# Loading four thirds of q, k and v ahead into hT's space, U by one DMA and TensorE, weight chunks in order of need, and batch 1 transposed on TensorE

## The chip, the cores and the metric

The kernel runs on one core of a Trainium2 chip. The metric is the device time of the whole kernel in microseconds (us); lower is better. Each kernel was timed in turns with the kernel before on the same chip.

The engines: TensorE (PE in the profile, PEld for its weight loads), VectorE (DVE), ScalarE (ACT), GpSimd (POOL) and SyncE (SP), which issues most DMAs. SBUF is the on-chip memory, PSUM the small memory that TensorE writes.

## The reference

Attention with normalised q and k, then a low-rank mixer over the sequence and a two-layer MLP with residual. Shapes: q, k, v are (8, 12, 448, 64); U is (448, 32), V (32, 448), w_ch1 (768, 3072), w_ch2 (3072, 768), all float32.

```python
q_n, k_n = rmsnorm(q, g_q), rmsnorm(k, g_k)
attn = softmax(q_n @ k_n.T / sqrt(64)) @ v       # per batch and head
x = attn.transpose(0, 2, 1, 3).reshape(8, 448, 768)
h = x.transpose(0, 2, 1) @ U @ V
u = x + h.transpose(0, 2, 1)
out = u + relu(u @ w_ch1) @ w_ch2
```

## The kernel before

The work on q, k and v goes by *thirds* (four heads of one batch; third `t` belongs to batch `t // 3`) and by *pairs* (two heads; pair `p` belongs to third `p // 2`). The *head* is the attention of batch 0, pairs 0 to 5, with the start of pair 6. Its loop has one step for each pair p, and the step for pair p also scales pair p + 2. After it, batch b's MLP fills TensorE while batch b+1's attention is woven in between. Six "chunks" each of w1 and w2 are loaded by GpSimd's queue.

```python
NE, NV, NWARM, NH = 2, 3, 16, 3
FA, FM, NPE = 0.77, 0.09, 8        # FA: the share of an MLP that the next attention is spread over
loads = ctx.enter_context(tc.tile_pool(name="loads", bufs=2))      # two thirds of q, k; two of v

def load_mix():                    # U, in 14 small DMAs
    Ur = moe_U.rearrange("(p j) r -> j p r", j=NJ)
    for par in range(2):
        for i, off in enumerate(OFFS[par]):
            lo, hi = max(off, 0), min(off + P, S)
            for j, p0, p1, r in segments(lo, hi):
                r += lo - off
                nc.sync.dma_start(Uf[r:r + p1 - p0, par, i, :], Ur[j, p0:p1, :])
    nc.sync.dma_start(Vf, ...)

def squares(t, hs=ALL, ss=(0, 1)):
    for s in ss:
        ...
        if t < 3:
            nc.scalar.activation(sqs[t, s][:, hs], qks[t][:, s, hs], AF.Square)
        else:
            nc.gpsimd.tensor_tensor(sqs[t, s][:, hs], qks[t][:, s, hs], qks[t][:, s, hs], OP.mult)

def scale(t, pr):                  # "the scaling": q and k times 1/rms, two VectorE instructions a pair
    ...
    for s in range(2):
        nc.vector.tensor_tensor(qkns[t][:, pr, s]..., qk[:, s, hp]...,
                                rstd[:, s, hp]....to_broadcast([SP, 2, NJ, D]), OP.mult)

def transposes(p):
    ...
    if p < NPE:                    # eight TensorE transposes and two evictions
        ...
    else:                          # one DMA transpose
        nc.sync.dma_start_transpose(qkT.rearrange("d s (j p) -> d (s j) p", j=NJ), qkn)
```

In the head's loop a third is loaded (`load(t + 3)`, `load_v(t + 3)`) when the buffer that it takes is free, and w1 chunks 2 to 5 go out at pairs 1 and 2. All six w2 chunks are issued together behind the head.

## Time and profile before

| | before |
|---|---|
| time, median of 3 runs | 659.18 us (659.03 to 661.39) |
| span of the profiled run | 659.2 us |
| TensorE busy | 599.2 us (91%) |
| first MLP matmul of batch 0 (the head's end) | 74.09 us |
| first matmul with w2 | 121.32 us |
| first MLP matmul of batch 1 | 154.28 us |
| from there to the end | 504.9 us |

Three lines of the page's second part: the span in 40 slices of 16.5 us. A digit is the busy share of a slice in tenths; PEclk is TensorE's granted clock in tenths of full speed; DMA is the mean busy share of the 16 DMA engines.

```profile
PE   5286895999999999899999999899999999999997
PEclk8688896999999999999999999999999999999999
DMA  6999697554443625564443534563444331030011
```

After the seventh slice TensorE is nearly always busy, so only the first 150 us have time to give. There the DMA engines are the busy ones. The timeline of TensorE (start in us, length, engine, line, what, count, and in brackets how long the engine had been idle and on whom it waited) shows the gaps:

```profile
20.37 0.40 PE L213 MATMUL sc<-qkT 64*112 64x448 bf16 x2 [0.92 <-ACT E_95 L218]
32.58 0.62 PE L213 MATMUL sc<-qkT 64*112 64x448 bf16 x2 [11.81 <-ACT E_95 L218]
...
50.65 1.04 PE L237 MATMUL o<-va_98,E_95 112*128 112x65 bf16 x16 [3.04 <-DVE t4b L296]
...
66.07 1.04 PE L237 MATMUL o<-va_99,E_95 112*128 112x65 bf16 x16 [3.98 <-DVE t4b L296]
...
74.09 1.14 PE L319 MATMUL ph<-u_367,w1b 128*128 128x384 bf16 x6
...
109.75 1.00 PE L213 MATMUL sc<-qkT 64*112 64x448 bf16 x4 [7.94 <-DVE qkT L205]
```

Gaps of 11.8, 3.0, 4.0 and 7.9 us. The bracket names the last engine in a chain, not the cause. The cause is in the chain of waits (start, length, what), followed back through the same time:

```profile
13.32 0.48 SPq L114
...
16.81 0.66 SPq L115
...
17.59 13.05 DMA qk<-in_q_dram
...
30.66 1.06 ACT sq L162
...
91.83 17.41 DMA qkT<-qkn
```

L114 is the line of U's 14 loads. Third 2 of q was issued at 17.59 us behind them and took 13.05 us to land; ScalarE's squares, and through them all that follows, waited for it. The last line is a DMA transpose of q and k that needed 17.41 us, issued while the six w2 chunks were loading.

### The profile page before, as it was taken

The numbers are of one execution on the slowest core, as the hardware profiler recorded it, in microseconds if no ns is written. First come the engines' busy times: TensorE is split into PE (matmuls) and PEld (weight loads), VectorE is DVE, ScalarE is ACT, GpSimd is POOL, SyncE is SP. The second block draws the span as 40 slices with busy tenths as digits, with TensorE's granted clock in tenths as the row PEclk, the third lists the DMA queues.
The fourth block names the chain that finished last, engine by engine and source line by source line (L and its number), as shares of the span: only waits on it lengthen the run. The fifth ranks groups of instructions, "written<-read, shape, count | busy, mean of one in ns | idle before, by whom it ended". The sixth has DMA issues, their size and how long they took to land.

```text
span 659.2 us, 11159 instructions
## 1 busy us (share of the span) xinstructions
PE 599.2 (91%) x4700; PEld 329.7 (50%) x4700; DVE 338.8 (51%) x737; ACT 233.9 (35%) x347; POOL 117.2 (18%) x96
## 2 busy tenths in 40 slices
PE   5286895999999999899999999899999999999997
PEld 2043452554445555554456555554456555554464
DVE  4257862664555546673645456673645456352211
ACT  4264252413553055414453056414543065402100
POOL 3024602220211202320220203320221200000000
PEclk8688896999999999999999999999999999999999
DMA  6999697554443625564443534563444331030011
GB/s 145 214 186 182 136 216 147 113 134 99 98 105 78 136 53 112 112 152 82 106 106 96 112 67 98 123 156 66 112 98 118 89 68 29 25 73 25 0 49 49
DMA packets 104534, 68.64 MB, mean 104 GB/s; under 512 B 60836, under 2 KB 100900, under 8 KB 104484
## 3 DMA queue, kind: packets, MB, share of 16 engines
q1 hardware_dynamic: 96292, 58.49, 39.0%
q0 software_dynamic: 7872, 9.44, 8.6%
q8 instruction: 37, 0.61, 0.4%
q14 instruction: 13, 0.11, 0.1%
q10 hardware_dynamic: 320, 0.00, 0.0%
HBM read 52.25 MB, written 11.01 MB: 96 GB/s over the span
## 4 chain that ended last, share of the span: by engine, by line
PE 77%; DMA 9%; DVE 8%; ACT 2%; issue 1%; SPq 1%; POOL 1%; DVEq 0%; POOLq 0%
PE po L334 32%; PE ph L319 30%; PE o L237 7%; PE sc L213 6%; DMA qk<-in_q_dram 4%; DVE qkn L184 3%; DMA qkT<-qkn 3%; DVE osb L338 1%; DMA vt<-in_v_dram 1%; DVE rstd L170 1%; PE pu L276 1%; ACT hT L322 1%; ACT E_96 L218 1%; DVE hT L324 1%; ACT E_95 L218 1%
## 5 line engine op out<-in xcount | busy, mean ns | idle before, releaser
L334 PE MATMUL po<-w2b,hT 128*128 128x384 bf16 x1344 | 235.2, 326 | 2.9 <-DVE osb L338 2.9
L334 PEld LDWEIGHTS <-hT 128*128 128x128 bf16 x1344 | 126.3, 98 | 92.5 <-issue 15.0
L319 PEld LDWEIGHTS <-w1b 128*128 128x128 bf16 x1152 | 106.7, 98 | 106.7 <-issue 17.6
L164 POOL TENSOR_TENSOR sq<-qk 112x1024 f32<-112x1024 f32 x42 | 79.0, 1896 | 370.9 <-DMA qk<-in_q_dram 354.0
L322 ACT ACTIVATE hT<-ph 128x384 bf16<-128x384 f32 (+1 forms) x96 | 52.3, 545 | 252.5 <-PE ph L319 252.5
L218 ACT ACTIVATE E_96<-sc 112x896 bf16<-112x896 f32 x96 | 85.6, 914 | 71.1 <-PE sc L213 71.1
L324 DVE TENSOR_SCALAR hT<-ph 128x384 bf16<-128x384 f32 (+1 forms) x96 | 59.8, 623 | 92.0 <-PE ph L319 91.4
L218 ACT ACTIVATE E_95<-sc 112x896 bf16<-112x896 f32 x96 | 85.4, 912 | 42.4 <-PE sc L213 42.3
L213 PE MATMUL sc<-qkT 64*112 64x448 bf16 x384 | 61.9, 384 | 29.9 <-DVE qkT L205 14.7
L184 DVE TENSOR_TENSOR qkn<-qk,rstd 112x512 bf16<-112x512 f32 x96 | 70.5, 774 | 17.9 <-ACT rstd L176 17.3
L170 DVE TENSOR_REDUCE rstd<-sq 112x16 f32<-112x1024 f32 (+1 forms) x50 | 58.2, 1167 | 23.8 <-ACT sq L162 15.5
L213 PEld LDWEIGHTS <-qkT 64*112 64x112 bf16 x384 | 21.5, 128 | 69.1 <-issue 56.8
L240 DVE RECIPROCAL rec<-o 128x4 f32<-128x4 f32 x96 | 17.2, 180 | 52.0 <-PE o L237 51.9
L237 PEld LDWEIGHTS <-E_95 112*128 112x128 bf16 x768 | 31.7, 101 | 16.1 <-issue 10.6
L237 PEld LDWEIGHTS <-E_96 112*128 112x128 bf16 x768 | 30.1, 98 | 11.8 <-DVE xs_100 L244 3.0
L319 PE MATMUL ph<-u_5020,w1b 128*128 128x512 bf16 x144 | 33.3, 379 | 0.0
L319 PE MATMUL ph<-u_1608,w1b 128*128 128x512 bf16 x144 | 33.3, 379 | 0.0
L319 PE MATMUL ph<-u_3314,w1b 128*128 128x512 bf16 x144 | 33.3, 379 | 0.0
L319 PE MATMUL ph<-u_6686,w1b 128*128 128x512 bf16 x144 | 31.2, 379 | 0.0
L319 PE MATMUL ph<-u_367,w1b 128*128 128x384 bf16 x144 | 28.1, 343 | 1.0 <-ACT hT L322 0.5
L319 PE MATMUL ph<-u_5889,w1b 128*128 128x384 bf16 x144 | 25.8, 326 | 0.0
L319 PE MATMUL ph<-u_2477,w1b 128*128 128x384 bf16 x144 | 25.6, 326 | 0.0
(100 smaller groups left out, 383.2 us busy)
## 6 DMA issues: line engine op xcount, KB each, us to landing
vt<-in_v_dram SPq DMA_DIRECT2D x24, 448.0 KB, 6.6
qk<-in_q_dram SPq DMA_DIRECT2D x23, 448.0 KB, 4.3
qk<-in_k_dram SPq DMA_DIRECT2D x23, 448.0 KB, 5.7
w1b<-in_moe_w_ch_dram POOLq DMA_DIRECT2D x6, 768.0 KB, 9.4
w2b<-in_moe_w_ch_dram POOLq DMA_DIRECT2D x6, 768.0 KB, 17.3
out_dram<-osb SPq DMA_DIRECT2D x8, 336.0 KB, 2.8
out_dram<-osb SPq DMA_DIRECT2D x8, 288.0 KB, 3.0
out_dram<-osb SPq DMA_DIRECT2D x8, 240.0 KB, 2.6
```

The source lines that it names most:

```text
L164: nc.gpsimd.tensor_tensor(sqs[t, s][:, hs], qks[t][:, s, hs], qks[t][:, s, hs], OP.mult)
L170: nc.vector.tensor_reduce(rstds[t][:, s, hs].rearrange("p h j -> p (h j)"), sqs[t, s][:, hs].rearrange("p h (j d) -> p (h j) d", d=D), AX, ...
L184: nc.vector.tensor_tensor(qkns[t][:, pr, s].rearrange("p j h d -> p h j d"), qk[:, s, hp].rearrange("p h (j d) -> p h j d", d=D), rstd[:, ...
L213: nc.tensor.matmul(sc[:, hh, 0:S], kT[pp, kc * SP:(kc + 1) * SP], qT[pp, :], start=True, stop=True)
L218: nc.scalar.activation(Es[p % NE][:, :, PAD + kc * S:PAD + (kc + 1) * S], scs.pop((p, kc))[:, :, 0:S], AF.Exp, scale=float(D) ** 0.5)
L237: nc.tensor.matmul(o[:, i, :], E[:, hh, c:c + P], va[:, hl, kc, :], start=(kc == 0), stop=(kc == NJ - 1))
L240: nc.vector.reciprocal(rec, o[:, :, D])
L276: nc.tensor.matmul(pu, lhsT, t4s[b][:, hs], start=True, stop=True)
L319: nc.tensor.matmul(ph, w1b[:, dc, hc * P:(hc + 1) * P], u[:, dc, :], start=(dc == 0), stop=(dc == KD - 1))
L322: nc.scalar.activation(hT[:, hc, 0:n], ph, AF.Relu)
L324: nc.vector.tensor_relu(hT[:, hc, 0:n], ph)
L334: nc.tensor.matmul(po, hT[:, hc, i * P:(i + 1) * P], w2b[:, hc, hs], start=(hc == 0), stop=(hc == KH - 1))
```

## The change

Its intent: to have data in SBUF before it is needed. While hT (the MLP's hidden layer, 24 KiB per partition) is unused in the head, thirds 2 and 3 are loaded into its space, so four thirds are issued at once. U comes by one DMA and is put in shape by TensorE transposes. w1 chunks go out one by one at pairs 1 to 4, w2 chunks three after the head and three at pairs 8 to 10. Pairs 8 to 11 (batch 1) are transposed on TensorE (NPE 12), and batch 1's attention is spread over half of batch 0's MLP (FA0 = 0.5) so that w2 may come later. Third 2's squares move from ScalarE to GpSimd, and one PSUM copy (mix_b) from VectorE to ScalarE.

```diff
+    spare = hT.rearrange("p k n -> p (k n)").bitcast(FP32).rearrange("p (t s h e) -> p t s h e", t=2, s=3, h=HG)
-    FA, FM, NPE = 0.77, 0.09, 8
+    FA, FM, NPE, FA0 = 0.77, 0.09, 12, 0.5
... (U: one DMA into Uf [112, 128]; setup_u and setup_v: cast, 4 + 8 TensorE transposes, two copies;
     the four small loads of g_q and g_k become two)
     def load(t, parts=1):
-        qks[t] = loads.tile([SP, 2, HG, NJ * D], FP32, tag="qk", name="qk")
+        if t in (2, 3):
+            qks[t] = spare[0:SP, t - 2, 0:2]
+        else:
+            qks[t] = loads.tile([SP, 2, HG, NJ * D], FP32, tag="qk", name="qk")
... (load_v the same)
-            if t < 3:
+            if t < 2:
                 nc.scalar.activation(sqs[t, s][:, hs], qks[t][:, s, hs], AF.Square)
             else:
                 nc.gpsimd.tensor_tensor(...)
... (mix_b)
-        nc.vector.tensor_copy(us[b][:, dc, :], pu)
+        nc.scalar.activation(us[b][:, dc, :], pu, AF.Copy)
... (attention)
-            if t + 2 < NT:
-                add(0, reduce, t + 2, ALL, (odd,))
+            if t + 2 < NT and p != 8:
+                add(0, reduce, t + 2, ALL, (0, 1) if p == 9 else (odd,))
+            if 8 <= p <= 10:
+                add(0, load_w2, p - 5)
... (head: loads first; pair 0 reordered; load(p + 4) at pairs 0 and 1)
         load(0, 2)
         load(1)
         load_v(0)
+        load(2)
+        load_mix()
+        load_v(1)
+        load_v(2)
+        load(3)
+        load_v(3)
         setup()
... (pair 0)
+                squares(1)
+                squares(2)
...
-            if p in (1, 2):
-                load_w1(2 * p)
-                load_w1(2 * p + 1)
+            if 0 < p < 5:
+                load_w1(p + 1)
... (main)
-        for i in range(6):
+        for i in range(3):
             load_w2(i)
-                weave(fill, total * FA, attention(b + 1) if b else rest)
+                weave(fill, total * (FA if b else FA0), attention(b + 1) if b else rest)
```

More of the change, by code (lines that the diff above doesn't have):

```diff
@@ L97, in setup, with setup_u, setup_v @@
             nc.gpsimd.memset(t, 0.0)
-        nc.gpsimd.memset(Uf, 0.0)
+        nc.gpsimd.memset(UT, 0.0)
         nc.gpsimd.memset(Vsh, 0.0)
-        for half in range(2):
-            nc.scalar.dma_start(gg[half * D:(half + 1) * D, :], g_q.rearrange("(d o) -> d o", o=1))
-            nc.scalar.dma_start(gk2[half * D:(half + 1) * D, :], g_k.rearrange("(d o) -> d o", o=1))
-    Uf = consts.tile([P, 2, 4, rank], FP32, name="Uf")
+        for t, g in ((gg, g_q), (gk2, g_k)):
+            nc.scalar.dma_start(t, g.rearrange("(a d o) -> a d o", a=1, o=1).to_broadcast([2, D, 1]))
+    Uf = consts.tile([SP, NJ * rank], FP32, name="Uf")
+    Uc = consts.tile([SP, NJ * rank], BF16, name="Uc")
+    UT = consts.tile([rank, PAD + S + PAD], BF16, name="UT")
     Vf = consts.tile([P, S], FP32, name="Vf")
     def load_mix():
-        Ur = moe_U.rearrange("(p j) r -> j p r", j=NJ)
+        nc.sync.dma_start(Uf, moe_U.rearrange("(p j) r -> p (j r)", j=NJ))
+        nc.sync.dma_start(Vf, moe_V.rearrange("r s -> () r s").to_broadcast([4, rank, S]))
+    def setup_u():
+        nc.vector.tensor_copy(Uc, Uf)
+        pt = ps_mm.tile([rank, S], BF16, tag="mm")
+        for j in range(NJ):
+            nc.tensor.transpose(pt[:, j * SP:(j + 1) * SP], Uc[:, j * rank:(j + 1) * rank], ident[:SP, :SP])
+        nc.vector.tensor_copy(UT[:, PAD:PAD + S], pt)
+    def setup_v():
+        pt = ps_mm.tile([P, 2, 4, rank], BF16, tag="mm")
         for par in range(2):
             for i, off in enumerate(OFFS[par]):
-                lo, hi = max(off, 0), min(off + P, S)
-                for j, p0, p1, r in segments(lo, hi):
-                    r += lo - off
-                    nc.sync.dma_start(Uf[r:r + p1 - p0, par, i, :], Ur[j, p0:p1, :])
-        nc.sync.dma_start(Vf, moe_V.rearrange("r s -> () r s").to_broadcast([4, rank, S]))
-    def setup_mix():
-        nc.vector.tensor_copy(Ub, Uf)
+                nc.tensor.transpose(pt[:, par, i, :], UT[:, PAD + off:PAD + off + P], ident[:rank, :rank])
+        nc.vector.tensor_copy(Ub, pt)
         nc.vector.tensor_copy(V4.rearrange("r (j p) -> r j p", j=NJ), Vf.rearrange("r (p j) -> r j p", j=NJ))
@@ L147, in load_v @@
         b, h0 = t // 3, (t % 3) * HG
-        vt = loads.tile([SP, HG, NJ * D], FP32, tag="vt")
+        if t in (2, 3):
+            vt = spare[0:SP, t - 2, 2]
+        else:
+            vt = loads.tile([SP, HG, NJ * D], FP32, tag="vt", name="vt")
         nc.sync.dma_start(vt, v[b, h0:h0 + HG].rearrange("h (p j) d -> p h (j d)", j=NJ))
@@ L396, in head @@
         reduce(0, A)
-        squares(0, Bh)
+        squares(0, Bh, (0,))
         rsqrt(0, A)
+        squares(0, Bh, (1,))
+        reduce(0, Bh, (0,))
         scale(0, 0)
@@ L401, in head @@
         transposes(0)
-        reduce(0, Bh)
+        reduce(0, Bh, (1,))
         rsqrt(0, Bh)
-        squares(1)
-        scale(0, 1)
-        load_mix()
-        load(2)
-        load_v(1)
-        load_v(2)
         cast_v(0)
@@ L412, in head @@
         load_w1(1)
+        scores(0, (0, 1))
         for p in range(7):
             t, odd = divmod(p, 2)
-            scores(p, (0, 1))
+            if p > 1:
+                scores(p, (0, 1))
             expo(p, 0)
@@ L418, in head @@
                 mix_a(0, p - 2)
+            if p == 0:
+                scale(0, 1)
             transposes(p + 1)
+            expo(p, 1)
             if p == 0:
-                reduce(1)
-            expo(p, 1)
-            if not odd:
+                squares(1)
+                squares(2)
+            elif not odd:
                 rsqrt(t + 1)
@@ L430, in head @@
                 mix_a(0, 5)
-            elif p < 6:
+            elif p:
                 heat(NH)
@@ L440, in head @@
                 mix_b(0, p - 2)
+            if p == 0:
+                scores(1, (0, 1))
+            expo(p, 3)
+            if p == 0:
+                reduce(1)
+                rsqrt(1)
             scale(t + 1, odd)
             if p == 1:
-                setup_mix()
-            squares(t + 2, ss=(odd,))
-            expo(p, 3)
-            reduce(t + 2, ss=(odd,))
+                setup_u()
+                setup_v()
+            if p > 1:
+                squares(t + 2, ALL, (odd,))
+            reduce(t + 2, ALL, (odd,))
+            if p < 2:
+                load(p + 4)
+                load_v(p + 4)
             if p < 6:
@@ L450, in head @@
                 cast_v(t + 1)
-                load(t + 3)
-                load_v(t + 3)
-            if p in (1, 2):
-                load_w1(2 * p)
-                load_w1(2 * p + 1)
+            if 0 < p < 5:
+                load_w1(p + 1)
     def mixing(b):
```

## The prediction

> **What bounds the kernel now.** From 154 us (batch 1's MLP starts, by the timeline) to the end TensorE is busy in 99 to 100% of nearly every slice (page, part 2); the change leaves those 505 us alone. Before that the core is starved. TensorE's timeline: warm-up until 10 us, the head (batch 0's attention) until 74 us, then batch 0's MLP with batch 1's attention until 154 us. The chain of waits runs here over DMA landings: U and v issues until 17.6 us, third 2 of q (13.05 us), 7.4 us (third 3), 7.6 us (third 4), 17.4 us (a DMA transpose). TensorE stands still 11.8 us at 20.8 to 32.6, about 3 us at 47, 4 us at 62, and 7.9 us at 102 to 110. The granted clock falls to 0.66-0.76 around them (windows of 10 us).
>
> Why the loads are late: 14 small U loads hold SyncE from 5.7 to 16.8 us, each waiting for an older DMA; thirds 3 and 4 are issued at 39.7 and 54.9 us, after a buffer is free. The DMA transposes of pairs 8 to 11 queue behind six w2 chunks issued together at 75.7 us.
>
> **What the change does.**
> - U: 14 loads become one; 12 TensorE transposes and small copies (each under 0.6 us) are added.
> - Thirds 0 to 3 issued by about 14 us; third 2 should land near 20 us instead of 31: most of the 11.8, 3 and 4 us stalls go. Its squares move to GpSimd (1.9 us each instead of 1.05).
> - mix_b's copy (0.54 us a pair) goes from VectorE, 97% busy at 50 to 60 us, to ScalarE.
> - Pairs 8 to 11: TensorE transposes (0.37-0.56 us a pair) and two evictions (0.45 + 0.38 us, for a 0.34 us gain). Removes the 7.9 us stall and some 3 us of slow clock.
> - w2 chunks are spread; batch 1's attention goes into the first half of batch 0's MLP. Neutral in TensorE work.
>
> **Floor.** In the first 120 us the queues took 56.6 us (47.2%) for 12 weight chunks and 46.4 us for eight thirds with the rest: 103 of 120 us. The Trainium skill, "DMA: Bandwidth & Descriptors" (Queues, rings and completion order) says that each DMA engine takes the queue rows in turn; the trace agrees: third 2, sharing with two w1 chunks, took 13.05 us against 3.4 us for the first loads. So the second matmul can't start before about 95 us (121 now).
>
> **Estimate.** Head: pair 2 starts near 31 us (39.5 now); pairs 2 to 6 need 5.2 us each (34.6 us now less 8.5 us of stalls): end at 57 us instead of 74. Batch 0's MLP part: 80 us less 8, 3 and about 1: 69 us, plus 0 to 4 us waiting for the last w2 chunk or third 7. Batch 1's MLP starts at 126 to 131 us instead of 154: 24 us won, nearly all critical.
>
> **Prediction: 635 us, 8 in 10 between 627 and 646.** Faster by over 2%: 0.91; within 2%: 0.08; slower: 0.01.
>
> **What would show it.** No TensorE gap above 4 us at 20 to 33 us; thirds 3 and 4 landed before use; VectorE busiest in the head, 5.2 us a pair; head end 54 to 62 us; no DMA transpose of q/k before 100 us; first po matmul at 96 to 106 us; last 505 us unchanged.
>
> **What would make it wrong.** Weight chunks delaying third 2 or 4 (head end near 65); GpSimd waiting for third 7 and so issuing the last w2 chunk late (5 to 10 us at the first po group); VectorE or ScalarE too dense when five pairs go into half the MLP; a slower steady state from shifted loads.

## More of the kernel before

One more reading, not looked at closely before the prediction, matters later: VectorE's time in the scalings (line L184 of this kernel), in two stretches, by the view of busy time by windows filtered to that line. The columns are window, length, VectorE's time with the count, clock, DMA share, GB/s.

```profile
0.00:74.10 74.10, 11.83 (x16) 0.79 0.85 173
74.10:142.00 67.90, 9.43 (x12) 0.92 0.80 161
```

28 scalings in 21.26 us.

## The result, and the profile after

The result is correct. The median is 644.41 us (643.31 to 645.25, 4 runs) against 659.11 us of the kernel before beside it: ratio 0.9768, 95% interval 0.9742 to 0.9795. A ratio here and below is the mean time of one kernel's runs over that of the other's runs of the same rounds, so not quite the ratio of the medians. Executions over 1.5% slower than the fastest of the same kernel are left out of the means. 14.7 us were won; 24 had been predicted. The time lies inside the stated range, near its slow end.

| | before | predicted | after |
|---|---|---|---|
| head's end | 74.1 us | 57 us | 62.6 us |
| from there to batch 1's MLP | 80.2 us | 69 to 73 us | 72.3 us |
| from there to the end | 504.9 us | the same | 506.6 us |
| span of the profiled run | 659.2 us | | 641.5 us |

(The traced execution of before took 661.1 us, one of its slower ones, that of after 643.3 us, its fastest, so the traces differ by 17.7 us, the medians by 14.7.)

The same lines of the page:

```profile
PE   5688988999999999899999999899999999999996
PEclk9689999999999999999999999899999999999999
DMA  9999797325346455444155355353355321040011
```

The DMA engines are busy without a break through the first four slices, and TensorE's second slice, a 2 before, is a 6. Its timeline:

```profile
28.55 0.37 PE L118 MATMUL pt<-ident,Uc 112*32 112x112 bf16 x4 [2.13 <-DVE Uc L115]
...
62.58 1.25 PE L333 MATMUL ph<-u_371,w1b 128*128 128x384 bf16 x6
...
85.53 0.55 PE L211 MATMUL pt<-ident,qkn 112*128 112x112 bf16 x8 [1.32 <-DVE hT L338]
...
100.90 2.11 PE L333 MATMUL ph<-u_371,w1b 128*128 128x384 bf16 x12 [1.62 <-DVE hT L338]
...
134.92 1.46 PE L333 MATMUL ph<-u_1558,w1b 128*128 128x512 bf16 x6
```

No gap is longer than 2.2 us after the start. All four gaps of before are gone. And yet the head ended 5.6 us later than estimated. The releaser in the brackets is VectorE now, and VectorE's scalings (L198 in this kernel) have become longer:

```profile
0.00:62.60 62.60, 18.83 (x17) 0.84 1.09 223
62.60:110.00 47.40, 13.39 (x12) 1.00 0.84 168
```

32.22 us for the same 28 scalings that took 21.26 us before (one lies across the border and is counted in both windows). In the chain of waits of the first 160 us the scalings are 15.1%; before it was 3.2%. Most of the DMA waits left the chain (the loads of q are 3.5% of it now, 17.6% before) and something that makes VectorE slow entered it. Line by line, in the head's step for pair 2, which scales pair 4 (one answer of the timeline, all engines, cut to GpSimd and the scaling; a pair's two scalings are one line):

```profile
35.90 1.88 POOL L178 TENSOR_TENSOR sq<-hT 112x1024 f32<-112x1024 f32 x1 [0.96 <-DMA hT<-in_k_dram]
...
36.09 3.68 DVE L198 TENSOR_TENSOR qkn<-hT,rstd 112x512 bf16<-112x512 f32 x2
...
37.74 1.49 POOL L167 CAST va_99<-hT 112x1024 bf16<-112x1024 f32 x1
```

The pair of scalings takes 1.27 to 1.29 us when alone and 3.68 us here. It started 0.2 us after GpSimd's square. 35.90 + 1.88 is 37.78: the first scaling seems to stand until the square ends, the second until the cast of v ends (37.74 + 1.49 = 39.23). This pattern fits the Trainium skill, "SBUF — State Buffer" (Who interferes with whom): "A DVE instruction with two SBUF inputs contends with a GpSimd instruction that reads SBUF", one engine holding a shared read interface for a whole instruction and the other blocked. The scaling has two SBUF inputs, q or k and rstd.

### The profile page after: what moved, and what is told of

Same layout as the page of the kernel before. It is cut to its first block, busy times and chain, and to the rows that moved or that the text cites. A ratio compares the mean times of both kernels' runs of the same rounds, so it can differ in the third digit from the quotient of the medians.

```text
span 641.5 us, 11220 instructions
## 1 busy us (share of the span) xinstructions
PE 599.3 (93%) x4741; PEld 330.7 (52%) x4741; DVE 349.7 (55%) x737; ACT 234.4 (37%) x351; POOL 122.1 (19%) x98
## 4 chain that ended last, share of the span: by engine, by line
PE 80%; DVE 13%; ACT 3%; DMA 2%; issue 1%; SPq 0%; DVEq 0%; ACTq 0%
PE po L348 33%; PE ph L333 29%; PE o L251 7%; PE sc L227 7%; DVE qkn L198 6%; DVE rstd L184 1%; DVE osb L352 1%; ACT E_95 L232 1%; PE pu L290 1%; DVE hT L338 1%; DMA qkT<-qkn 1%; DMA qk<-in_q_dram 1%; PE warm L509 1%; PE pt L211 1%; ACT E_96 L232 1%
## 5 line engine op out<-in xcount | busy, mean ns | idle before, releaser
L348 PEld LDWEIGHTS <-hT 128*128 128x128 bf16 x1344 | 127.3, 98 | 93.6 <-issue 15.8
L333 PEld LDWEIGHTS <-w1b 128*128 128x128 bf16 x1152 | 105.9, 98 | 105.8 <-issue 16.6
L178 POOL TENSOR_TENSOR sq<-qk 112x1024 f32<-112x1024 f32 x40 | 75.4, 1892 | 353.6 <-DMA qk<-in_q_dram 317.9
L232 ACT ACTIVATE E_96<-sc 112x896 bf16<-112x896 f32 x96 | 85.9, 913 | 65.7 <-PE sc L227 65.7
L198 DVE TENSOR_TENSOR qkn<-qk,rstd 112x512 bf16<-112x512 f32 x88 | 71.4, 851 | 16.5 <-ACT rstd L190 16.0
## 6 DMA issues: line engine op xcount, KB each, us to landing
w1b<-in_moe_w_ch_dram POOLq DMA_DIRECT2D x6, 768.0 KB, 15.1
```

Of the source, the lines that this page charges most:

```text
L198: nc.vector.tensor_tensor(qkns[t][:, pr, s].rearrange("p j h d -> p h j d"), qk[:, s, hp].rearrange("p h (j d) -> p h j d", d=D), rstd[:, ...
L232: nc.scalar.activation(Es[p % NE][:, :, PAD + kc * S:PAD + (kc + 1) * S], scs.pop((p, kc))[:, :, 0:S], AF.Exp, scale=float(D) ** 0.5)
L333: nc.tensor.matmul(ph, w1b[:, dc, hc * P:(hc + 1) * P], u[:, dc, :], start=(dc == 0), stop=(dc == KD - 1))
L348: nc.tensor.matmul(po, hT[:, hc, i * P:(i + 1) * P], w2b[:, hc, hs], start=(hc == 0), stop=(hc == KH - 1))
```

## The experiments

The theory: in the kernel before, GpSimd's squares came when a late load had just landed, and VectorE was mostly idle then, waiting for the same load. With the loads early, GpSimd's reads fall on VectorE's scalings, and VectorE, which sets the pace of the head, stands still for them. The rivals: (1) the scalings are slow because thirds 2 and 3 lie in hT's space; (2) the denser DMA traffic slows VectorE; (3) GpSimd being busy at all slows it. A second question is what each part of the change is worth: the head's part (early loads, U, w1 order) and the second part (TensorE transposes of batch 1, w2 spread, FA0).

Runs of one batch ran on the same chip: the first four below, the next four, the last four.

### The head's part alone

```diff
-    FA, FM, NPE, FA0 = 0.77, 0.09, 12, 0.5
+    FA, FM, NPE, FA0 = 0.77, 0.09, 8, 0.77
-            if t + 2 < NT and p != 8:
-                add(0, reduce, t + 2, ALL, (0, 1) if p == 9 else (odd,))
+            if t + 2 < NT:
+                add(0, reduce, t + 2, ALL, (odd,))
-            if 8 <= p <= 10:
-                add(0, load_w2, p - 5)
-        for i in range(3):
+        for i in range(6):
             load_w2(i)
```

> The head's part of the change alone (early loads, U by one DMA, weight order, w1 spread, mix_b's copy on ScalarE); pairs 8 to 11 again by DMA transposes, w2 chunks all issued at once, batch 1's attention over 0.77 of batch 0's MLP. Theory (the two parts add up): the head ends at about 62.6 us as in the full change, so 11 us are won there, and the stall behind the w2 chunks (7.9 us before) comes back: 648 to 651 us. Rival (the head's gain is given back later because the loads collide with w2): over 654 us. If the second part is worth nothing: 644 us.

Measured: 644.33 us, ratio 0.9759 (0.9742 to 0.9777): no slower than the whole change. In its trace the head ends at 58.6 us, 4 us sooner than in the trace of the whole change although the head's code is the same, and the scalings meet GpSimd at other places (3.34 us at 18, 3.20 at 46, 5.00 at 58). The last of them does not fit the pattern wholly (GpSimd's line L140 issues the six w2 chunks):

```profile
56.03 4.52 POOL L140 DMA_DIRECT2D w2b<-in_moe_w_ch_dram  x6
58.04 5.00 DVE L198 TENSOR_TENSOR qkn<-qk,rstd 112x512 bf16<-112x512 f32 x2
60.53 1.95 POOL L178 TENSOR_TENSOR sq<-qk 112x1024 f32<-112x1024 f32 x1
```

The pair's first scaling takes 2.04 us although GpSimd only issues weight chunks beside it. Elsewhere scalings beside such issues take 0.67 us (at 42.4 us in the run with the squares of thirds 3 to 7 on ScalarE, for one). What held this one is not shown. The wait for the DMA transpose came back, but smaller:

```profile
92.27 0.59 PE L227 MATMUL sc<-qkT 64*112 64x448 bf16 x4 [3.12 <-DVE qkT L219]
```

3.1 us, not 7.9. So the head's part carries the gain, and the second part adds nothing that these two results can tell apart. My expectation of 648 to 651 us was wrong.

### The second part alone, on the kernel before

```diff
-    FA, FM, NPE = 0.77, 0.09, 8
+    FA, FM, NPE, FA0 = 0.77, 0.09, 12, 0.5
+            (the reduce, load_w2 and weave lines of the change)
```

> The second part alone on the kernel before: pairs 8 to 11 transposed on TensorE, w2 chunks spread over pairs 8 to 10, attention of batch 1 pressed into the first half of batch 0's MLP. Theory: the head still ends at 74 us, and the 80 us after it become about 72, as in the full change: 651 to 653 us. Rival (it only pays when the w1 chunks are early): 656 to 660 us.

Measured: 658.35 us, 0.9966 (0.993 to 1.0002): at most a little faster. The 7.9 us gap at 102 us is gone from its trace, but the stretch from the head's end (74.3 us) to batch 1's MLP (151.8 us) is 77.5 us against 80.2: three of its pairs of scalings take 4.1 to 4.4 us (at 75, 98 and 113 us), while no pair in the kernel before took more than 2.15 before 110 us. What the part takes out of the DMA waits it gives back, for the most part, in VectorE's waits.

### Squares of thirds 2 to 7 on ScalarE

```diff
-            if t < 2:
+            if t < 8:
                 nc.scalar.activation(sqs[t, s][:, hs], qks[t][:, s, hs], AF.Square)
```

> The changed kernel with the squares of thirds 2 to 7 on ScalarE (1.05 us each) instead of GpSimd (1.9 us each). Theory (GpSimd reading SBUF holds up VectorE's scaling, which has two SBUF inputs): the 28 scalings before 110 us take 19 to 21 us in sum instead of 32.2 (28 at 0.65 would be 18), the head ends 3 to 6 us sooner, total 636 to 642 us. Rival 1 (scalings that read third 2 and 3 from hT's space are slow for their place): those 8 keep a median near 1.4 us. Rival 2 (DMA writes slow VectorE): all stay near 32 us in sum. If ScalarE's 13 us more become the limit: scalings short, yet 644 us or more.

Measured: 640.52 us, 0.9709 (0.9681 to 0.9736). The same view of the scalings:

```profile
0.00:60.40 60.40, 10.77 (x17) 0.86 1.11 226
60.40:110.00 49.60, 8.07 (x12) 0.97 0.79 168
```

The 14 pairs of scalings before 110 us take 18.8 us: thirteen of them 1.27 to 1.30 us, one 2.14 (beside a cast of v, which stays on GpSimd). Those that read hT's space are as short as the others, which is against rival 1. The DMA engines' share in the head is no lower (1.11 against 1.09), which is against rival 2. The head ends at 60.4 us only, because ScalarE does third 2's squares ahead of pair 0's exponentials now and TensorE waits 5.6 us for those at 20 us. In total the run is faster than the change's first ratio (0.9768), but its interval overlaps that of the change's second run below (0.9734, 0.9701 to 0.9766): that the shorter scalings win time here is likely, not settled.

### The scaling's second input in PSUM

rstd is put in the unused end of the PSUM bank of o. GpSimd keeps all its work.

```diff
+    ob = ps_o.tile([P, 512], FP32, tag="o", name="ob")
-            rstds[t] = norm.tile([SP, 2, HG, NJ], FP32, tag="rstd", name="rstd", bufs=3)
+            c = 384 + 32 * (t % 3)
+            rstds[t] = ob[0:SP, c:c + 32].rearrange("p (s h j) -> p s h j", s=2, h=HG)
-            o = ps_o.tile([P, 4, D + 1], FP32, tag="o")
+            o = ob[:, 0:4 * (D + 1)].rearrange("p (c e) -> p c e", c=4)
```

> The changed kernel with the scaling's second input (rstd) in PSUM, in the unused end of the bank of o; GpSimd does what it did. Theory (the two SBUF inputs are what collides): the 28 scalings take 18 to 21 us in sum instead of 32.2 although GpSimd's squares run at the same times, the head ends 3 to 6 us sooner, total 635 to 641 us. Rival 1 (place in hT) and rival 2 (DMA writes): sum stays near 32 us, total 644 us. Rival 3 (GpSimd busy at all slows VectorE): stays near 32 us too.

Measured: 647.3 us, 0.9799 (0.9778 to 0.9821), slower than the change's two runs (644.41 and 643.43 us; all four executions are above all eight of those); but the scalings did what the theory said. The same two views (scalings by windows; the timeline at the same place):

```profile
0.00:62.00 62.00, 11.17 (x18) 0.83 1.10 226
62.00:110.00 48.00, 6.72 (x11) 1.00 0.82 160
```

```profile
35.04 1.88 POOL L179 TENSOR_TENSOR sq<-hT 112x1024 f32<-112x1024 f32 x1 [1.07 <-DVE rec L256]
...
35.40 1.27 DVE L200 TENSOR_TENSOR qkn<-hT,ob 112x512 bf16<-112x512 f32 x2
```

The scalings start in the middle of GpSimd's square and take 1.27 us, as if alone. This is no matter of luck in timing: 12 of the 28 overlap a square or a cast of GpSimd in this trace (10 in the changed kernel's first trace, most of them stretched, up to 3.74 us). All 28 together take 17.89 us, each between 668 and 689 ns, with the same DMA share (1.10 in the head), the same place in hT and the same GpSimd work. That leaves none of the three rivals: what collides is the second SBUF input. This is the cleanest of the runs for the mechanism.

The time was lost elsewhere, in part before and in part after 110 us. The view of waits up to 110 us (engine, tile and line, waited for whom: us in total, times, longest) has lines that the changed kernel has no match for:

```profile
PE ob L253 <- ACT ob L192: 6.4, 5, 1.8
...
PE ob L253 <- DVE ob L186: 2.9, 4, 1.4
PE ob L253 <- DVE qkn L200: 2.1, 3, 0.8
```

o and rstd share one tile now, and TensorE's write of o waits for engines that only work on rstd: 11.4 us in sum. The cure for one wait made another. A further 3.3 us are lost from batch 1's MLP to the end (509.9 us in this trace against 506.6 in the changed kernel's first); their cause was not looked for.

### The changed kernel once more

No edit.

> The changed kernel once more, unedited, to have it on the same chip as the next three and to see a second trace. Theory (GpSimd's reads meet VectorE's scalings whenever a load happens to land just before one): the sum of the 28 scalings before 110 us differs from the first trace's 32.2 us by some us and the head's end moves with it, between 58 and 63 us; the time stays at 0.975 to 0.979 of before. Rival (the collisions are fixed by the program): the same pairs collide, sum within 1 us of 32.2, head end 62 to 63 us.

Measured: 643.43 us, 0.9734 (0.9701 to 0.9766), single runs from 640.35 to 644.81. The head ends at 57.6 us in this trace, 5 us sooner than in the first, from the same program; head's end and ratio lie just outside what I expected (58 to 63 us, 0.975 to 0.979). The place of the collision shown above looks like this here:

```profile
36.82 3.04 POOL L178 TENSOR_TENSOR sq<-hT 112x1024 f32<-112x1024 f32 x1 [1.00 <-DVE x L255]
36.83 1.27 DVE L198 TENSOR_TENSOR qkn<-hT,rstd 112x512 bf16<-112x512 f32 x2
```

The two start within 0.01 us and now it is GpSimd that takes longer: 3.04 us instead of 1.88, by about the 1.2 us of the scalings. So a shift of a fifth of a microsecond goes with a change of who waits. The skill's page says that issue order, not the shape of the operation, decides who blocks. These traces agree that the same two operations can end either way, but their recorded starts do not show the order: here the square is recorded first, by 0.01 us, and yet waits, and the scaling at 93.90 us below is recorded 0.72 us ahead of a square and takes 4.16 us. GpSimd was off the critical path there, so when it loses, nothing is lost: in the steps for pairs 2 to 5 the scalings all take 1.27 us in this trace and the head is 5 us shorter. In the second stretch this execution was less lucky: 5.55 us for the pair at 75.75 us, behind two squares and a cast in a row, and 4.76 us for the one at 93.9. Head's end to batch 1's MLP is 75.7 us against 72.3. The sum of scalings is 29.1 us.

### Squares of thirds 3 to 7 on ScalarE, third 2 on GpSimd

```diff
-            if t < 2:
+            if t < 8 and t != 2:
```

> The changed kernel with the squares of thirds 3 to 7 on ScalarE and those of third 2 left on GpSimd (ScalarE is needed for pair 0's exponentials then). Theory: sum of the scalings 20 to 22 us (one collision of about 2.5 us at 18 us stays), pairs 2 to 6 of the head 5.2 to 5.4 us each, head end 57 to 59 us, total 2 us below the run with all squares of thirds 2 to 7 on ScalarE: 0.967 to 0.970 of before. Rival (the head is no longer bound by VectorE): head end near 60.4 us as in that run and 0.971.

Measured: 641.0 us, 0.970 (0.968 to 0.972). The sum of scalings is 20.7 us, with one collision left (4.01 us at 18 us), pairs 2 to 6 of the head are 5.3 us apart as estimated from the kernel before (5.2), and the head ends at 59.3 us, 1.1 us sooner than with all of them on ScalarE. One trace of each does not settle 1.1 us, and the totals (0.970 and 0.9709) can't be told apart.

### The same with batch 1's attention over 0.6 of batch 0's MLP

```diff
-    FA, FM, NPE, FA0 = 0.77, 0.09, 12, 0.5
+    FA, FM, NPE, FA0 = 0.77, 0.09, 12, 0.6
```

> The same with batch 1's attention over 0.6 instead of 0.5 of batch 0's MLP. Theory (between 62 and 110 us TensorE waits because VectorE is 88% busy when five pairs are pressed into half the MLP): TensorE's idle time from the head's end to batch 1's MLP falls from about 6 us to 3 us, total 2 to 3 us under sq_act37, 0.963 to 0.967 of before. Rival (w2 chunks, issued with pairs 8 to 10, come later than the second matmul now): a wait of 3 us or more at the first po group, same or slower than sq_act37.

Measured: 637.54 us, 0.9652 (0.9634 to 0.967), 3.5 us under the run with 0.5 by the medians. The stretch after the head is 71.5 us against 73.3, and no wait for w2 shows at the first matmul with w2 (101.6 us). So 0.6 is better than 0.5, but not by the way I expected: without the collisions VectorE was only 73% busy there with 0.5 (37.3 of 50.7 us), and what TensorE waited for most was ScalarE's exponentials (3.1 us, now 1.6). TensorE's idle time in the stretch fell from 5.4 to 4.4 us, not to 3, and the two traced executions differ by 1.1 us only; where the rest of the 3.5 us was won is not shown. (0.77 with the change's w2 order was refused by the check before any run: w2 would be read before its last chunk is issued.)

### The U part alone, on the kernel before

```diff
-  (14 DMAs of U, cast to Ub)
+  (setup_u, setup_v and load_mix of the change)
```

> The U part alone on the kernel before: one DMA, TensorE transposes, copies; order of the other loads, buffers and NPE as before. Theory (the 14 small loads held the issue of third 2 from 7 to 17.6 us): third 2 is issued near 7 us and lands before 21 us, the TensorE gap of 11.8 us at 20.8 us falls below 4 us, the 3 and 4 us gaps at thirds 3 and 4 stay, since those loads still wait for a buffer: 7 to 9 us faster, 0.986 to 0.989 of before. Rival (w1 chunks are what makes third 2 late): gap still over 8 us, 0.995 to 1.0.

Measured: 653.56 us, 0.9883 (0.9836 to 0.993). The size was as expected, the way there was not. Third 2 was issued at 14.77 us, not at 7, because its buffer is third 0's and is free only when pair 1 has been scaled:

```profile
13.18 1.54 DVE qkn L191
...
14.77 5.30 DMA qk<-in_q_dram
```

So the U loads (and V behind them) held it for 2.8 us only (17.59 less 14.77; within the trace of the kernel before pair 1's scaling ends at 15.25 us, which makes it 2.3). But those 2.8 us were the ones in which GpSimd issued two w1 chunks (14.6 to 16.5 us in the kernel before) and SyncE the load of V: here the first chunk went out at 14.10 us, the second at 15.11 and V long before. Issued between the chunks, third 2 landed in 5.30 us; behind both, V and the last U loads in 13.05. Which of these counts for how much is not shown. The gap at 20.8 us shrank from 11.8 us to 1.8. The head ended at 65.7 us. The 3 us gap at third 3 went, that at third 4 stayed (3.7 us), and TensorE waited 3.2 us at 28 us for U's cast, which it did not before. The gap behind the w2 chunks stayed (8.64 us at 94 to 102 us).

### All squares of thirds 2 to 7 on ScalarE, third 2's placed later

```diff
-            if t < 2:
+            if t < 8:
...
                 squares(1)
-                squares(2)
...
                 rsqrt(1)
+                squares(2)
...
-    FA, FM, NPE, FA0 = 0.77, 0.09, 12, 0.5
+    FA, FM, NPE, FA0 = 0.77, 0.09, 12, 0.6
```

> Squares of thirds 2 to 7 all on ScalarE, those of third 2 placed after pair 0's exponentials and the next rsqrt (ScalarE idled 5.6 us there), attention of batch 1 over 0.6 of batch 0's MLP. Theory: the collision at 18 us (4.2 us for a pair of scalings instead of 1.3) goes too, sum of the 28 scalings 18 to 19 us, head end 56.5 to 58.5 us, total 2 to 3 us under the last best: 0.960 to 0.964 of before. Rival (the exponentials of pair 1, now 2 us later, hold up the head as much): head end near 60 us, 0.965.

Measured: 634.13 us (632.51 to 635.13), 0.9594 (0.9569 to 0.962), correct. The scalings:

```profile
0.00:55.20 55.20, 10.95 (x18) 0.90 1.10 227
55.20:110.00 54.80, 7.05 (x11) 0.97 0.88 182
```

17.99 us in sum, no collision left; the head ends at 55.2 us, batch 1's MLP starts at 126.4. In the chain of waits of the first 160 us the scalings are 2.4%. Against the change's two ratios (0.9768 and 0.9734) that is 9 to 11.5 us of 660, with the same loads as in the change. Not all of it is the collisions: FA0 differs too. Against the run with 0.6 and third 2's squares on GpSimd (0.9652, 0.9634 to 0.967) only those two squares differ, and with them the one collision left (4.22 us for that pair instead of 1.29): the head ends 4.8 us sooner (55.2 against 60.0) and the ratio falls by 0.6% with intervals apart.

### The same with 0.66

> The same with 0.66. Theory (attention and the last w2 chunk move together, since chunk 5 is issued with pair 10): TensorE has less VectorE work per time in the first half, 1 us more gained. Rival: the second matmul now starts so soon after chunk 5's issue that TensorE waits 3 to 6 us for it; then slower than with 0.6.

Measured: 632.88 us (631.3 to 636.66), 0.9587 (0.9542 to 0.9632). The intervals of the two overlap almost wholly: 0.66 is no worse and not shown to be better. TensorE shows no wait over 1.2 us between 26 us and batch 1's MLP but one (1.23 us at 54 us), so the rival's wait for w2 did not come.

### The head's part alone, squares of thirds 3 to 7 on ScalarE

The edit of the first experiment together with `t < 8 and t != 2`.

> The head's part of the change alone (as the earlier run of it) with the squares of thirds 3 to 7 on ScalarE: what the second part (TensorE transposes of pairs 8 to 11, w2 spread, attention in half the MLP) is worth when collisions no longer blur it, against 0.970 with the second part. Theory (the second part removes a 3 us wait for a DMA transpose and was masked by collisions it brought itself): 0.973 to 0.976. Rival (it is worth nothing once third 2 to 4 are early): 0.968 to 0.971.

Measured: 642.61 us, 0.9728 (0.9704 to 0.9751). With the second part the same squares gave 0.970 (0.968 to 0.972), in another batch. The wait for a DMA transpose is 6.2 us in this trace (at 86 to 92 us). So with the collisions mostly out of the way the second part looks worth about 0.3%, 2 us; the intervals overlap, so this is likely and not settled.

### The changed kernel with U by 14 loads

> The changed kernel with U by 14 small DMAs and casts as before, at the place in the queue that the one DMA has. Theory (small DMAs hold SyncE, each waits for an older one): v of third 1 and 2 and third 3 are issued 6 to 10 us later, pair 2 waits for v or third 3, head end 64 to 68 us, 0.982 to 0.988 of before. Rival (with third 2 already issued ahead of them the small loads cost nothing): 0.973 to 0.977.

The result of this kernel is wrong, and by my mistake, not on purpose: in the changed order the loads come ahead of GpSimd's clearing of U's tile, so the clearing, which waits 18.6 us for them, zeroes U. The mistake also changes the timing. GpSimd's queue is held until 22.1 us, and with it the first cast of v (22.6 us instead of 14.0) and the first two w1 chunks (issued from 23.6 us instead of 15.0). It ran in 638.51 us, 0.966 (0.9638 to 0.9683), faster than the change, with the head's end at 58.7 us and no collision at 17 us (1.29 us for that pair). SyncE was held by the U loads from 6.9 to 20.8 us, and the head was no longer for it. So my expectation (0.982 to 0.988) fell. Whether small loads cost nothing once third 2 is ahead of them, or whether the later w1 chunks paid for them, this run can't tell; the share of the U part within the whole change stays open.

### All runs beside each other

Scalings: the sum over the first 28 (14 pairs), which end before about 110 us.

| kernel | median us | ratio to before | head's end | batch 1's MLP | scalings us |
|---|---|---|---|---|---|
| before | 659.1 | 1 | 74.1 | 154.3 | 21.3 |
| after, first trace | 644.4 | 0.9768 | 62.6 | 134.9 | 32.2 |
| after, second trace | 643.4 | 0.9734 | 57.6 | 133.3 | 29.1 |
| squares 2 to 7 on ScalarE | 640.5 | 0.9709 | 60.4 | 134.3 | 18.8 |
| rstd in PSUM | 647.3 | 0.9799 | 62.0 | 136.6 | 17.9 |
| squares 3 to 7 on ScalarE | 641.0 | 0.970 | 59.3 | 132.6 | 20.7 |
| the same, FA0 0.6 | 637.5 | 0.9652 | 60.0 | 131.5 | 20.9 |
| squares 2 to 7, later, FA0 0.6 | 634.1 | 0.9594 | 55.2 | 126.4 | 18.0 |
| the same, FA0 0.66 | 632.9 | 0.9587 | 57.1 | 126.9 | 18.5 |
| head's part alone | 644.3 | 0.9759 | 58.6 | 136.1 | 26.8 |
| the same, squares 3 to 7 on ScalarE | 642.6 | 0.9728 | 58.1 | 135.8 | 20.9 |
| second part alone | 658.4 | 0.9966 | 74.3 | 151.8 | 27.6 |
| U part alone | 653.6 | 0.9883 | 65.7 | 146.1 | 21.6 |
| U by 14 loads (wrong result) | 638.5 | 0.966 | 58.7 | 131.3 | 23.4 |

(Where batch 1's attention is spread over 0.77 of the MLP, or the head ends late, the 28 scalings go on longer, to 136 us in the kernel before.)

## Why the prediction was right, and where it was off

The time (635, range 627 to 646) was right within its range, and the direction with it. The gain of 24 us was mis-sized: 14.7 us by the first medians, 16.7 by the second batch's. That the time stayed inside the range is owed to the width of the range: what cost the difference was not in the sum.

- *The loads bound the head, and loading early takes those gaps away.* Right. The gaps of 11.8, 3.0 and 4.0 us are gone, and most of the DMA waits left the chain. The DMA transposes of q and k begin at about 100 us (the first at 100.3, in the second trace at 98.7), and batch 1's MLP to the end stayed within 2 us (506.6 and 505.3 us against 504.9).
- *"14 small U loads hold SyncE from 5.7 to 16.8 us".* True as read, but only 2.3 to 2.8 us of it held third 2; its buffer was not free before about 15 us. The U part alone is still worth 1.2%; the likely reason, argued from two traces, is that in those 2.8 us the w1 chunks got in front.
- *"Thirds 0 to 3 issued by about 14 us".* The last of them was issued by about 24 us. Third 2's q landed early as said (15.8 us), but third 3's q and k only at 32.1 and 35.8 us, not before use: GpSimd's squares waited for them. VectorE never waits for the result of those squares in the changed kernel's head, but the late landing set when they ran: the square that collides at 35.90 us was released by it.
- *"So the second matmul can't start before about 95 us"*, and "first po matmul at 96 to 106 us". It started at 107.4 us in the first trace and 105.8 in the second; the earliest of all runs is 96.5. That fits a floor near 95 us but does not show one. The 3.4 us that the prediction set beside third 2's 13.05 are those of halves of 224 KB; a whole q of a third with no weight chunk under way took 4.17 us (issued at 69.57 us in the kernel before).
- *"Pairs 2 to 6 need 5.2 us each … end at 57 us".* This is the step that failed in the first trace. 5.2 us was read from a kernel in which scalings and squares rarely met. What the sum lacked is the cost of their meeting: 32.2 us for the 28 scalings instead of 17.9 (with rstd in PSUM), that is 14 us, against 3.4 us in the kernel before. The prediction did list GpSimd's longer squares (1.9 us), but as work off the critical path. In the second trace, in which GpSimd lost the first meeting, the head did end at 57.6 us; without collisions pairs are 5.3 us apart.
- *"Pairs 8 to 11: … Removes the 7.9 us stall and some 3 us of slow clock" and "Neutral in TensorE work".* Over-sized. The second part alone gave 0.3%, with an interval that touches zero, and nothing visible on top of the head's part; once collisions are out, about 2 us. The stall was smaller anyway after early loads (3.1 and 6.2 us in two traces), and pressing five pairs into half of the MLP made VectorE dense (88% busy from 62.6 to 110 us, the stands counted; 73% where the squares are on ScalarE) and full of collisions (6 us of the 14). The prediction had named a VectorE or ScalarE too dense there as a risk, without a size. Spreading the pairs over 0.6 won 3.5 us.
- *The estimate as a whole* was nearly exact for a kernel without collisions: that kernel has its head's end at 55.2 us, batch 1's MLP at 126.4 and 634.1 us, against the predicted 57, 126 to 131 and 635. (It also has 0.6 instead of 0.5, so part of this agreement is luck.)

## What to carry to other kernels

When a change removes the waits for data, ask which engines will now run at the same time that never did before: a duration read from the old trace holds only for the neighbours it had there. Before you give GpSimd an operation that reads SBUF, look whether VectorE has instructions with two SBUF inputs on the critical path, and prefer ScalarE for it if ScalarE has room. And when two executions of one program differ by several microseconds in the same stretch, look for the first place where they part, and for the engine whose instruction grew longer there.

## What the Trainium skill lacked or had wrong

- "SBUF — State Buffer" (Who interferes with whom) has the rule that explains this, and the traces agree with its part on two SBUF inputs. It quotes two slowdowns as factors, but has no time for such a pair of instructions: here a pair of VectorE instructions of 0.67 us each took up to 5.55 us, since GpSimd had two squares (1.9 us each) and a cast (1.04 us) in a row. It also does not say how little it takes: here a shift of 0.2 us went with a change of who waits, and the two traces of one program are 5 us apart at the head's end. The recorded starts do not tell who issued first (a scaling 0.72 us ahead of a square, and yet 4.16 us long).
- The same page (Summary: rules for kernel authors) advises to schedule whichever engine is off the critical path; it does not name moving one of the two SBUF inputs to PSUM as a cure, though that follows from what it says of instructions with at most one SBUF input. It took the collision away fully (28 scalings in 17.89 us, none over 689 ns), at the price of 11.4 us of waits where rstd shared a PSUM tile with a matmul output.
- "DMA: Bandwidth & Descriptors" (Queues, rings and completion order) says that the DMA engines take queue rows in turn. It gives no figure for what a transfer loses when it comes second: the same third of q took 5.30 us when issued at 14.77 us, between two w1 chunks, and 13.05 us in the kernel before, issued 2.8 us later, behind both.
